# Where a fused transformer block waits for its transfers: waits on other products, queries in fewer transfers, and one PSUM bank used less

## The chip, the cores and the metric

The kernel runs on one core of a Trainium2 chip. The core has TensorE (PE; its weight loads are listed apart as PEld), VectorE (DVE), ScalarE (ACT), GpSimd (POOL) and SyncE (SP, which here does nothing but issue DMAs). TensorE writes its results to PSUM, whose banks (128 partitions of 512 fp32 values) are handed out by name. The metric is the device time of one launch in microseconds, and lower is better. A profiled execution comes with each kernel; its span is the time from its first instruction to its last, a little less than the time of the launch.

## The reference

One transformer block with adaptive layer norm: 2048 rows of 512 values, 32 attention heads of 16 with one shared key and value head, and an MLP of width 1376, all in fp32.

```python
sa, ca, ga, sb, cb, gb = split(silu(c) @ w_mod)            # six rows of 512
h = layernorm(x) * (1 + ca) + sa
q = (h @ wq) as 32 heads of 16;  k = h @ wk;  v = h @ wv   # one k, v of 16 for all heads
p = softmax(q k^T * 16 ** -0.5)
x = x + ga * ((p v) @ wo)
h = layernorm(x) * (1 + cb) + sb
x = x + gb * (gelu(h @ w1 + b1) @ w2 + b2)
```

## The kernel before, in words

**Numbers.** TensorE takes operands in a reduced fp32 format. Where that is not enough a value is split into a high and a low part and three products are summed (high x high, low x high, high x low). Queries lie in DRAM in such parts (`dq`), and a unit's query tile `qst` holds in each of its two halves (partitions 0 to 63 and 64 to 127, the index `s`): 16 partitions high, 16 low, 16 high again, and two with the negated row maxima (48, 49). The keys `ks` are laid out to match, so that one product with 64 rows sums all three, and subtracts the maximum too.

**Attention.** The rows come in 8 blocks of 256, and each block's heads in 8 groups of four. That makes 64 units. For each unit there are three kinds of product on TensorE:
- max products `m` (L490; 2048 in all, 32 a unit): scores with the queries as rows, which VectorE reduces to row maxima (L495). They run ahead of the unit that needs them. `put_max` turns the maxima, and its `send` (L534) writes them by four DMAs into rows 48 and 49 of the unit's `qst`;
- exp products `e` (L584; 2048): scores with the keys as rows, on which ScalarE takes the exponential (L587) into `p`;
- probability products `acc` (`pv`, L598; 4096, in four column groups): `va` times `p`. A row of ones in `va` yields the sums of the softmax.

`load_q` (L461, L463) fetches a later unit's queries, six DMAs of 16 partitions each and two (L463) that set the maxima's rows; there are four `qst` tiles. It is called when half of an earlier unit's max products are reduced.

**Order.** The engines run the instructions in the order in which the Python code writes them. The main loop passes over each unit's key tiles in pairs X, Y. Each pass has two half-steps: in one the e products of the half s = 1 lead, in the other the rest, and between them `end_step` issues a burst of 16 acc products of the pair before. A counter `clock` advances four times in a pass, so a half-step is two ticks. `later(n, fn)` puts a piece of code off by n ticks, `due()` runs what has come due.

**Filling.** Into the half-steps goes other work: the query projections of later blocks, and for each finished block the rest of the layer (`rest`): the attention output times wo (`wops`), the transposes of its normalised rows (`tp`), the MLP's first product (`w1ps`) and second (`w2ps`). These are generators in `queue`. A job yields the batch of products for the next half-steps, or a number of ticks until it wants to go on (`go_on`, `advance`, `take`). `rest` yields 8 ticks ahead of the transposes and 4 ahead of w1, so that the statistics on other engines can be finished; other waits of it are shorter. A half-step without filling is written by `plain`.

**PSUM.** Max products have three banks (tag `m`), e products one each of `e0`, `e1`, `e2`, acc one (`v`), and one bank, `x`, is the filling's. In a half-step without filling `plain` puts the last max product of one of its halves into `x`:

```python
if not holder and mp.has(t) and n > 1:
    other[-1] = 1.0, lambda: mp.step(t, tag="x", bufs=1)
```

**Attention output.** `fetch_half` (L717, L719) fetches a half block's output, four pairs of DMAs into the tile `os` (the output, and the softmax sums' reciprocals `drs`). Seven ticks later `norm` multiplies them on GpSimd (L733) and splits the product into `onH`, `onL` (L134). SP executes its DMAs in order; a DMA whose tile isn't free holds all behind it.

**Weights.** w1 is fetched anew for each block in pieces of 512 KB (`fetch_w1`, L747, three tiles `w1t`), three of them when `fetch_rest` runs (with the block's x, L753). `prep_w2` loads w2 once in pieces `w2f` (L1074), which GpSimd splits. `heed` notes a w1 piece with a tick, six later than its issue; `wait_early` makes an e product (one in every fourth tick, s = 0, odd pairs) wait for the first piece whose tick has come, so that the products of w1 themselves wait for less.

## Time and profile before

| | |
|---|---|
| median of 3 runs | 1591.61 us (1591.12 to 1593.79) |
| the profiled execution | 1592.94 us |
| its span | 1590.6 us |
| mean granted TensorE clock | 0.996 of full speed |
| PE busy | 1563.0 us (98%) |
| PEld busy | 1008.8 us (63%) |
| DVE busy | 1410.8 us (89%) |
| ACT busy | 1201.1 us (76%) |
| POOL busy | 667.5 us (42%) |

Times are microseconds. A group's row gives the line, engine, operation, the tiles out<-in and their shapes, then the count, the busy time and the mean of one instruction in nanoseconds, and behind it the idle time of the engine ahead of these instructions with what ended most of it. A row of the waits, "PEld m L490 <- DVE mx L495: 145.2, 363, 1.4", says who waited, for whom, for how many us, how often, and the longest. A row of the timeline begins with the time from the span's start and a duration; "x2" means that it holds two instructions in a row, and the bracket holds the idle time ahead of it and what ended it. PEq and SPq are the sequencers of PE and SP: an EVENT_SEMAPHORE there is a wait in an instruction of its own, and a DMA_DIRECT2D is a DMA being issued. Matmuls overlap one another and their ends are modelled, so the start of a weight load is the better mark of when TensorE went on.

### The profile page before, as it was taken

The page shows a single profiled execution, that of the slowest core. Times are in us where ns is not written, and L with a number is a line of the kernel's source. Part 1 is how long each engine was busy: PE and PEld are TensorE (multiplying, and loading weights), DVE is VectorE, ACT ScalarE, POOL GpSimd, SP SyncE. Part 2 cuts the span into 40 slices and gives each one's busy share as a digit, 9 for nine tenths or more (in the row PEclk, how much of TensorE's full clock was granted, in tenths as well). Part 3 has the DMA queues.
Part 4 walks back from the last instruction along what each step waited for, and adds up shares of the span by engine and source line. Part 5 has one row for each costly group of instructions (what it writes and reads, how often), then busy time and mean ns, then how long its engine had stood idle before and what let it go on. Part 6 is the DMA issues. An engine that isn't in the chain of part 4 may idle for free.

```text
span 1590.6 us, 41519 instructions
## 1 busy us (share of the span) xinstructions
PE 1563.0 (98%) x16369; PEld 1008.8 (63%) x16369; DVE 1410.8 (89%) x2473; ACT 1201.1 (76%) x2393; POOL 667.5 (42%) x1176
## 2 busy tenths in 40 slices
PE   6999999999999999999999999999999999999998
PEld 3466665557665676657666676656666576656667
DVE  7899999899999998999989999999999999999615
ACT  5577778778777887778877887778877787778853
POOL 4445434747422571246421462244612473225711
PEclk8999999999999999999999999999999999999999
DMA  7236312313020220303112120303112120212231
GB/s 250 82 113 214 105 68 70 128 39 101 17 98 31 68 69 25 103 18 107 32 49 79 54 85 22 106 14 98 43 37 89 45 96 19 95 39 63 81 134 73
DMA packets 83126, 121.62 MB, mean 76 GB/s; under 512 B 19614, under 2 KB 56222, under 8 KB 82676
## 3 DMA queue, kind: packets, MB, share of 16 engines
q1 hardware_dynamic: 82916, 118.97, 23.0%
q8 instruction: 129, 2.11, 0.6%
q14 instruction: 65, 0.53, 0.1%
q10 hardware_dynamic: 16, 0.00, 0.0%
HBM read 91.13 MB, written 27.27 MB: 74 GB/s over the span
## 4 chain that ended last, share of the span: by engine, by line
PE 88%; DVE 4%; POOL 4%; ACT 2%; DMA 1%; issue 1%; SPq 0%; POOLq 0%; DVEq 0%; ACTq 0%
PE acc L598 29%; PE m L490 21%; PE e L584 17%; PE w1ps L183 8%; PE w2ps L183 4%; DVE mx L495 3%; PE wops L183 2%; POOL xh L805 2%; PE qps L183 2%; PE w2ps L177 1%; PE w1ps L177 1%; ACT p L587 1%; PE tp L183 1%; PE kps L159 1%; POOL x L809 0%
## 5 line engine op out<-in xcount | busy, mean ns | idle before, releaser
L495 DVE TENSOR_REDUCE mx<-m 128x1 f32<-128x512 f32 x2048 | 1270.1, 681 | 101.4 <-PE m L490 73.8
L587 ACT ACTIVATE p<-e 128x512 f32<-128x512 f32 x2048 | 1067.2, 599 | 308.0 <-PE e L584 240.2
L490 PE MATMUL m<-ks,qst 64*128 64x512 f32 x2048 | 819.6, 424 | 6.1 <-ACT ks L393 2.3
L584 PE MATMUL e<-qst,ks 64*128 64x512 f32 x2048 | 739.1, 409 | 3.4 <-ACT p L587 1.5
L598 PE MATMUL acc<-p,va 128*32 128x256 f32 x8192 | 548.8, 385 | 0.0
L490 PEld LDWEIGHTS m<-ks,qst 64*128 64x128 f32 x2048 | 362.8, 184 | 168.8 <-DVE mx L495 145.2
L584 PEld LDWEIGHTS e<-qst,ks 64*128 64x128 f32 x2048 | 366.0, 184 | 91.2 <-ACT p L587 64.2
L598 PEld LDWEIGHTS acc<-p,va 128*32 128x32 f32 x8192 | 213.9, 109 | 218.9 <-issue 115.6
L183 PE MATMUL w1ps<-h2H,w1t 64*128 64x256 f32 x1232 | 236.7, 288 | 0.8
L539 POOL TENSOR_SCALAR mt<-turned 8x32 f32<-8x32 f32 x256 | 53.4, 209 | 400.6 <-DVE turned L545 388.6
L183 PEld LDWEIGHTS w1ps<-h2H,w1t 64*128 64x128 f32 x1232 | 184.1, 185 | 32.8 <-issue 23.3
L183 PE MATMUL w1ps<-h2L,w1t 64*128 64x256 f32 x616 | 169.6, 275 | 0.0
L183 PE MATMUL w2ps<-w2H,gH 64*128 64x512 f32 x286 | 118.0, 413 | 0.0
L183 PE MATMUL w2ps<-w2L,gH 64*128 64x512 f32 x286 | 117.3, 410 | 0.0
L183 PE MATMUL w2ps<-w2H,gL 64*128 64x512 f32 x286 | 117.3, 410 | 0.0
L183 PEld LDWEIGHTS w1ps<-h2L,w1t 64*128 64x128 f32 x616 | 113.5, 184 | 0.0
L906 POOL TENSOR_SCALAR tt<-tt 128x256 f32<-128x256 f32 x77 | 31.2, 405 | 162.5 <-ACT tt L905 159.3
L907 POOL TENSOR_TENSOR tt<-tt,z 128x256 f32<-128x256 f32 x77 | 57.1, 741 | 6.4
L134 POOL TENSOR_TENSOR gL<-z,gH 128x256 fp32r<-128x256 f32 x77 | 56.9, 739 | 6.4
L917 POOL TENSOR_TENSOR z<-tt,z 128x256 f32<-128x256 f32 x77 | 56.3, 731 | 6.0
L916 POOL TENSOR_TENSOR tt<-tt,z 128x256 f32<-128x256 f32 x77 | 56.8, 737 | 0.0
L183 PEld LDWEIGHTS w2ps<-w2H,gH 64*128 64x128 f32 x286 | 52.7, 184 | 5.9 <-DVE ot L953 2.5
(188 smaller groups left out, 1468.0 us busy)
## 6 DMA issues: line engine op xcount, KB each, us to landing
w1t<-dw SPq DMA_DIRECT2D x82, 512.0 KB
qst<-dq SPq DMA_DIRECT2D x384, 32.0 KB
do<-oc SPq DMA_DIRECT2D x64, 128.0 KB
dw<-w1s SPq DMA_DIRECT2D x11, 512.0 KB
xt<-in_A_x_dram SPq DMA_DIRECT2D x4, 1024.0 KB
dq<-qH SPq DMA_DIRECT2D x16, 256.0 KB
dq<-qL SPq DMA_DIRECT2D x16, 256.0 KB
x<-in_A_x_dram SPq DMA_DIRECT2D x8, 512.0 KB
```

What stands on the lines that cost most here:

```text
L134: eng_l.tensor_tensor(out=dst_l, in0=src, in1=raw(dst_h), op=ALU.subtract)
L177: nc.tensor.matmul(ps, a, b_, start=first_, stop=last_)
L183: nc.tensor.matmul(ps, a[rows], b_[rows], start=first_ and s == 0, stop=last_ and s == 1)
L490: nc.tensor.matmul(m, qsts[u][rows, j, t * P:(t + 1) * P], ks[rows, kc * 512:(kc + 1) * 512], start=True, stop=True)
L495: nc.vector.tensor_reduce(out=self.mx[u][:, i, kc:kc + 1], in_=m, axis=AX.X, op=ALU.max)
L539: nc.gpsimd.tensor_scalar(out=mt[:, g:g + 32], in0=turned[g:g + 4 * T, :], scalar1=1.0, scalar2=0.0, op0=ALU.mult, op1=ALU.add)
L584: ins = nc.tensor.matmul(e, ks[rows, kt * P:(kt + 1) * P], rhs, start=True, stop=True)
L587: nc.scalar.activation(ptiles[u, K][:, j, s, :], e, AF.Exp, scale=0.25)
L598: nc.tensor.matmul(accs[u][32 * cidx:32 * cidx + 32, :], va[:, kt, :], rhs, start=kt == 0, stop=kt == NKT - 1)
L907: nc.gpsimd.tensor_tensor(out=tt, in0=tt, in1=z, op=ALU.mult)
L916: nc.gpsimd.tensor_tensor(out=tt, in0=tt, in1=z, op=ALU.mult)
L917: nc.gpsimd.tensor_tensor(out=z, in0=tt, in1=z, op=ALU.add)
```

## The change

- The list of noted transfers and `wait_early` now cover the queries (6 ticks for s = 1, 8 for s = 0), the rows of the maxima (5) and the w1 pieces (8, the first three of a block 24). Acc products take the waits, one transfer each, in place of e products; the first acc product of a burst's first key tile takes none. `wait_early` looks for any noted transfer whose tick has come, where it looked only at the first.
- `load_q` fetches a half's queries in two DMAs in place of three: the low parts first, then the high part, written to both of its places by one DMA. The half s = 1 comes first, also where the maxima are sent.
- `fetch_half` fetches two head groups at once, and the other two four ticks later.
- A job in `queue` has a mark for a yield of over one tick. In `plain`, no max product goes to the bank `x` while a job so marked is due within two ticks.

```diff
@@ -448,6 +448,21 @@
     NU = len(units)
     qsts = {}
 
+    heeded = []
+    def heed(dma, n):
+        if not draining[0]:
+            heeded.append((clock[0] + n, dma))
+    def wait_early(ins):
+        for one in heeded:
+            if one[0] <= clock[0]:
+                heeded.remove(one)
+                tc.add_manual_dep(ins.ins, one[1].ins.name, mybir.DependencyInfo(mybir.DependencyClass.Sync, mybir.DependencyReason.DATA),
+                                  reason="a transfer that a product needs soon")
+                break
     def load_q(u):
 
         b, Q = units[u]
@@ -456,11 +471,14 @@
         h, g, a0 = r0 // BQ, Q // 2, (Q % 2) * 2
         cols = slice(r0 % BQ, r0 % BQ + w)
         assert (h, g) in sent
-        for s in range(2):
-            for r, part in ((0, 0), (16, 1), (32, 0)):
-                nc.sync.dma_start(out=raw(qst[64 * s + r:64 * s + r + 16]), in_=dq[h][g][part, a0 + s][:, :, cols])
+        for s in (1, 0):
+            low, high = (dq[h][g][part, a0 + s][:, :, cols] for part in (1, 0))
+            n = 6 if s else 8
+            heed(nc.sync.dma_start(out=raw(qst[64 * s:64 * s + 16]), in_=low), n)
+            heed(nc.sync.dma_start(out=raw(qst[64 * s + 16:64 * s + 48]), in_=high.unsqueeze(0).to_broadcast([2, 16, 2, w])), n)
             if u >= QBUFS:
-                nc.sync.dma_start(out=raw(qst[64 * s + 48:64 * s + 50]), in_=dz)
+                heed(nc.sync.dma_start(out=raw(qst[64 * s + 48:64 * s + 50]), in_=dz), n)
 
     class Max:
 
@@ -527,11 +545,11 @@
         ml = att.tile([4 * T, P], F32R, name=f"ml{u}", tag="ml", bufs=2)
 
         def send():
-            for s in range(2):
+            for s in (1, 0):
                 for r, src in ((48, mh), (49, ml)):
                     dst = qst[64 * s + r:64 * s + r + 1].rearrange("p j (t n) -> p (j t) n", n=P)
                     ring = nc.scalar if u == 0 and s else nc.sync
-                    ring.dma_start(out=raw(dst), in_=raw(src[2 * T * s:2 * T * (s + 1), :].unsqueeze(1)))
+                    heed(ring.dma_start(out=raw(dst), in_=raw(src[2 * T * s:2 * T * (s + 1), :].unsqueeze(1))), 5)
             placed.add(u)
 
         def gather():
@@ -554,20 +572,6 @@
 
     ptiles = {}
     accs = {}
-    heeded = []
-
-    def wait_for(ins, other, reason):
-        tc.add_manual_dep(ins.ins, other.ins.name, mybir.DependencyInfo(mybir.DependencyClass.Sync, mybir.DependencyReason.DATA),
-                          reason=reason)
-
-    def heed(dma, n):
-
-        heeded.append((clock[0] + n, dma))
-
-    def wait_early(ins):
-        if heeded and heeded[0][0] <= clock[0]:
-            wait_for(ins, heeded.pop(0)[1], "a weight piece")
-
     def sexp(u, K, j, s, bank):
 
         w = blocks[units[u][0]][1]
@@ -581,9 +585,7 @@
             kt, rhs = K, qst[rows, j, :]
         else:
             kt, rhs = 2 * K + j, qst[rows].rearrange("p j n -> p (j n)")
-        ins = nc.tensor.matmul(e, ks[rows, kt * P:(kt + 1) * P], rhs, start=True, stop=True)
-        if clock[0] % 4 == 2 and s == 0 and K % 2:
-            wait_early(ins)
+        nc.tensor.matmul(e, ks[rows, kt * P:(kt + 1) * P], rhs, start=True, stop=True)
         nc.scalar.activation(ptiles[u, K][:, j, s, :], e, AF.Exp, scale=0.25)
 
     def pv(u, K):
@@ -595,8 +597,10 @@
             for cidx in range(4):
                 s, j = divmod(cidx, 2)
                 rhs = pt[:, j, s, :] if w == 512 else pt[:, kt - 2 * K, s, j * w:(j + 1) * w]
-                nc.tensor.matmul(accs[u][32 * cidx:32 * cidx + 32, :], va[:, kt, :], rhs,
-                                 start=kt == 0, stop=kt == NKT - 1)
+                ins = nc.tensor.matmul(accs[u][32 * cidx:32 * cidx + 32, :], va[:, kt, :], rhs,
+                                       start=kt == 0, stop=kt == NKT - 1)
+                if kt % 2 or cidx:
+                    wait_early(ins)
 
     def finish_unit(u):
         b, Q = units[u]
@@ -712,11 +716,17 @@
         def fetch_half(hf):
             os_ = att.tile([P, 2, KD, HQ], F32, name=f"os{b}_{hf}", tag="opk", bufs=1)
             cols = slice(hf * HQ, (hf + 1) * HQ)
-            for g in range(KD):
-                src = do[b][2 * g:2 * g + 2, :, 0:16, cols].rearrange("q c r n -> (q c) r n")
-                nc.sync.dma_start(out=os_[:, 0, g, :], in_=src)
-                src = drs[b][8 * g:8 * g + 8, cols].unsqueeze(1).to_broadcast([8, 16, HQ])
-                nc.sync.dma_start(out=os_[:, 1, g, :], in_=src)
+            def fetch_heads(gs):
+                for g in gs:
+                    src = do[b][2 * g:2 * g + 2, :, 0:16, cols].rearrange("q c r n -> (q c) r n")
+                    nc.sync.dma_start(out=os_[:, 0, g, :], in_=src)
+                    src = drs[b][8 * g:8 * g + 8, cols].unsqueeze(1).to_broadcast([8, 16, HQ])
+                    nc.sync.dma_start(out=os_[:, 1, g, :], in_=src)
+            fetch_heads(range(KD // 2))
+            later(4, lambda: fetch_heads(range(KD // 2, KD)))
             oss[hf] = os_
             later(7, lambda: norm(hf))
 
@@ -744,7 +754,7 @@
 
     def fetch_w1(b, w1ts, f):
         w1ts[f] = wts_pool["rest"].tile([P, 2, KD, P], F32R, name=f"w1t{b}_{f}", tag="w1t", bufs=3)
-        heed(nc.sync.dma_start(out=raw(w1ts[f]), in_=dw1[f]), 6)
+        heed(nc.sync.dma_start(out=raw(w1ts[f]), in_=dw1[f]), 8 if f > 2 else 24)
 
     def fetch_rest(b):
 
@@ -1094,6 +1104,7 @@
             held.append(r)
         else:
             job[0] = clock[0] + max(abs(r), 1)
+            job[2] = r > 1
         return r is not None
 
     def resume():
@@ -1109,7 +1120,7 @@
                 break
 
     def put_off(*jobs):
-        queue.extend([0, job] for job in jobs)
+        queue.extend([0, job, False] for job in jobs)
 
     def take():
         advance()
@@ -1310,7 +1321,9 @@
                 a, b_, c_, d = banks
                 one = mixture(exps(s, [(K, 0, a), (K, 1, c_)]), maxes(s, n))
                 other = maxes(t, n)
-                if not holder and mp.has(t) and n > 1:
+                soon = any(planned and time <= clock[0] + 2 for time, _, planned in queue)
+                if not holder and not soon and mp.has(t) and n > 1:
                     other[-1] = 1.0, lambda: mp.step(t, tag="x", bufs=1)
                 issue(one, exps(t, [(K, 0, b_)]) + other + exps(t, [(K, 1, d)]))
 
```

In the built program the instructions of PE, DVE, ACT and POOL other than waits stand in the same order before and after (12,137 matmuls). SP issues 996 DMAs in place of 1124. On PE the waits in instructions of their own fall from 420 to 40, and 672 acc products have a wait for a DMA. The max products in bank `x` fall from 62 to 34: the 28 that move are four in each of the blocks 0 to 6, in the two half-steps without filling ahead of the transposes and the two ahead of w1.

## The prediction

> **What bounds the kernel now.** I read the page first (busy shares, chain), then the waits of TensorE's weight loads, then the instructions of single half-steps.
>
> ```profile
> span 1590.6 us, 41519 instructions
> PE 1563.0 (98%) x16369; PEld 1008.8 (63%) x16369; DVE 1410.8 (89%) x2473; ACT 1201.1 (76%) x2393; POOL 667.5 (42%) x1176
> PE 88%; DVE 4%; POOL 4%; ACT 2%; DMA 1%; issue 1%; SPq 0%; POOLq 0%; DVEq 0%; ACTq 0%
> L495 DVE TENSOR_REDUCE mx<-m 128x1 f32<-128x512 f32 x2048 | 1270.1, 681 | 101.4 <-PE m L490 73.8
> ```
>
> TensorE is busy 98% of the span and is 88% of the chain; VectorE, reducing the max products, follows at 89%. The work of neither is changed: the built program holds the same instructions on PE, DVE, ACT and POOL in the same order, on 12,137 matmuls. What changes is which PSUM bank 28 of the max products use, what TensorE waits for, and what SP issues when. So the time can change only where TensorE or VectorE stands still, and such places must be found one by one.
>
> ```profile
> PEld m L490 <- DVE mx L495: 145.2, 363, 1.4
> L490 PEldq EVENT_SEMAPHORE  x256: 51/51/692, 29.0 to 1478.0; - x128
> L584 PEldq EVENT_SEMAPHORE  x128: 51/51/1089, 76.5 to 1515.4; - x128
>   DMA w1t<-dw: 3.5, 4
> ```
>
> Most of the waiting is for a max product's bank: 145.2 us of weight-load idle, in 363 places. The two semaphore lines are waits in instructions of their own, for the query transfers, 51 ns at the median. The last row, of the exp products' line, is the only wait for a transfer that any probability-loop product shows: 3.5 us in four times, for w1 pieces.
>
> **Transfer waits moved to probability products (acc, L598).** In the built program separate semaphore instructions on PE fall from 420 to 40, and 672 acc products carry one wait each. If all 380 were on the path, 380 x 0.051 = 19.4 us would go. Two neighbouring pairs of half-steps of one shape tell otherwise:
>
> ```profile
> 801.81 0.59 PEld L598 LDWEIGHTS acc<-p,va 128*32 128x32 f32 x16 [0.24 <-issue]
> 804.67 0.16 PEld L598 LDWEIGHTS acc<-p,va 128*32 128x32 f32 x8 [0.26 <-issue]
> 813.33 0.59 PEld L598 LDWEIGHTS acc<-p,va 128*32 128x32 f32 x16 [0.24 <-PE e L584]
> 816.19 0.16 PEld L598 LDWEIGHTS acc<-p,va 128*32 128x32 f32 x8 [0.26 <-issue]
> ```
>
> The half-step from 801.81 has no extra waits, that from 813.33 has four: 2.86 us both. I count the removal at 0; the cover is the matrix work already queued, and without it the price would be those 51 ns each. The four w1 waits go: 24 ticks of 1.43 us (half a 2.85 us half-step) stand between an early piece and its wait. That is -3.5, of which 2.18 belongs to block 0, below; the rest is **-1.3**. The other new waits are 5 to 8 ticks, 7 to 11 us, behind the place where SP is given the transfer. Before has no wait for query rows anywhere, so I take 0, except where SP itself is late (block 0). 128 fewer issues help SP, which bounds nothing.
>
> **The bank left alone (x).** Max products have three banks of their own (m), and in steps without filling the third product of a step takes the filling's bank x. After the change 28 of 62 don't: four in each of blocks 0 to 6, in the two half-steps ahead of the transposes (tp) and the two ahead of w1. Block 1, ahead of tp:
>
> ```profile
> 504.86 0.59 PEld L598 LDWEIGHTS acc<-p,va 128*32 128x32 f32 x16 [0.24 <-issue]
> 506.53 0.18 PEld L490 LDWEIGHTS m<-ks,qst 64*128 64x128 f32 x1 [0.15 <-DVE mx L495]
> 507.13 0.18 PEld L490 LDWEIGHTS m<-ks,qst 64*128 64x128 f32 x1 [0.41 <-DVE mx L495]
> 507.56 0.59 PEld L598 LDWEIGHTS acc<-p,va 128*32 128x32 f32 x16 [0.24 <-issue]
> 510.18 0.59 PEld L598 LDWEIGHTS acc<-p,va 128*32 128x32 f32 x16 [0.24 <-issue]
> 511.38 0.18 PEld L183 LDWEIGHTS tp<-ident,xh 64*128 64x128 f32 x1 [0.61 <-POOL x L809]
> 504.63 8.01 DVE L495 TENSOR_REDUCE mx<-m 128x1 f32<-128x512 f32 x13
> ```
>
> VectorE runs without a break here, 13 reductions in 8.01 us, 0.62 each. The third product (506.53) sits in x, the fourth (507.13) takes the m bank that was just reduced. Without x the third takes the bank freed at 507.13 and the fourth the next, one reduction later: the acc of 507.56 moves by **+0.60**. In the next half-step the fourth product needs the reduction of that step's own first. Its load then stands at about 510.65 instead of 509.52, the acc burst 0.43 behind it (507.13 to 507.56) at 511.08, against 510.18 + 0.60: **+0.30**. In return tp needs no reduction of x: its load stands 1.20 us behind its acc, where other bursts stand 1.00 (813.33's kind): **-0.20**.
>
> Ahead of w1:
>
> ```profile
> 524.64 0.59 PEld L598 LDWEIGHTS acc<-p,va 128*32 128x32 f32 x16 [0.24 <-issue]
> 525.75 0.19 PEld L490 LDWEIGHTS m<-ks,qst 64*128 64x128 f32 x2
> 525.99 0.41 PEld L490 LDWEIGHTS m<-ks,qst 64*128 64x128 f32 x2
> 526.82 0.18 PEld L584 LDWEIGHTS e<-qst,ks 64*128 64x128 f32 x1 [0.42 <-ACT p L587]
> 527.25 0.59 PEld L598 LDWEIGHTS acc<-p,va 128*32 128x32 f32 x16 [0.25 <-issue]
> 528.41 0.18 PEld L183 LDWEIGHTS w1ps<-h2H,w1t 64*128 64x128 f32 x1 [0.57 <-issue]
> 526.41 0.69 DVE L495 TENSOR_REDUCE mx<-m 128x1 f32<-128x512 f32 x1 [0.38 <-PE m L490]
> ```
>
> The fourth product's load moves behind the first's reduction, which ends at 526.41 + 0.69 = 527.10: load about 527.14, acc at 527.57, **+0.30** on 527.25. The half-step before it has a wait for ACT at this place that covers nearly all: **+0.05**. The w1 load loses its wait for x: 1.16 us behind its acc to 1.00, **-0.16**. Together 0.60 + 0.30 - 0.20 + 0.05 + 0.30 - 0.16 = 0.89 us a block, times 7 blocks = **+6.2**. Bounds: 0 if TensorE's delay only fills time in which VectorE bounds anyway; 1.25 a block, +8.8, if tp and w1 gain nothing.
>
> **Attention output fetched in two parts, block 0.** Heads 2 and 3 of the fetch are issued four ticks later, behind the queries and w2.
>
> ```profile
> 279.22 0.57 SPq L719 DMA_DIRECT2D os<-drs  x1
> 284.73 0.84 SPq L1074 DMA_DIRECT2D w2f<-in_B_w_dram  x2
> 284.44 0.74 POOL L733 TENSOR_TENSOR os<-os 128x256 f32<-128x256 f32 x1 [0.92 <-DMA os<-drs]
> 286.40 2.38 POOL L134 TENSOR_TENSOR onL<-os,onH 128x1024 fp32r<-128x1024 f32 x1
> 292.12 3.68 SPq L1074 DMA_DIRECT2D w2f<-in_B_w_dram  x2
> 296.33 1.40 SPq L747 DMA_DIRECT2D w1t<-dw  x3
> 297.85 0.68 SPq L534 DMA_DIRECT2D qst<-mh  x1
> DMA  0696889999669796899999999831320000000020
> ```
>
> The last issue moves from 279.22 to some 283.1 (two parts of queries, now three issues each, and w2f ahead of it), so GpSimd's fourth product, 284.44, and all behind it come between 0 (if that lateness is absorbed) and 3.9 us later; I take 2.5, since this product now also waits 0.92 us for its transfer, but others precede it. SP's second w2f fetch (292.12) waits for GpSimd, and behind it on SP stand x, three w1 pieces and the max rows of the next unit but one (297.85). The last row is DMA use in 40 slices of 296 to 308 us: it falls to nothing at slice 31, 305. So the max rows land near 305 before, near 307.5 after.
>
> ```profile
> 301.90 0.18 PEld L584 LDWEIGHTS e<-qst,ks 64*128 64x128 f32 x1 [1.43 <-DMA w1t<-dw]
> 303.18 0.22 PEld L584 LDWEIGHTS e<-qst,ks 64*128 64x128 f32 x2 [0.75 <-DMA w1t<-dw]
> 304.25 0.20 PEld L598 LDWEIGHTS acc<-p,va 128*32 128x32 f32 x8 [0.65 <-issue]
> 303.30:306.70 3.40, 3.40 (x21) 1.40 (x23) 1.57 (x3) 1.09 (x2) 3.23 (x4) 0.50 0.24 74
> 306.28 0.33 PEld L584 LDWEIGHTS e<-qst,ks 64*128 64x128 f32 x1
> ```
>
> Before, the w1 waits of 1.43 + 0.75 = 2.18 us hold the max rows' users back far enough. Without them the acc burst of 304.25, which now carries the max rows' waits, comes at 302.07 and stands until 307.5: 5.4 us in place of 2.18, **+3.2**. Everything of TensorE is queued behind it. Bounds: +0.7 if the rows land at 305.0, +4.6 if 3.9 us later. The windows row has the granted clock at 0.50 for 3.40 us behind those idles (columns: length, five engines' busy time, clock, DMA share, GB/s); running half as fast it loses up to 1.7 us, and I keep it: 0, bounds -1.7 and +1.7.
>
> The first product that reads those rows is the exp product at 306.28, 2.03 us behind the acc burst; a wait there would hide 2.03 of the 5.4 us, and leave +1.2.
>
> The Trainium skill ("DMA: Bandwidth & Descriptors", Rules for kernel authors) advises to issue a transfer early and to wait on its semaphore late, after the work that can be done meanwhile. That speaks against this change: with the wait left at the last place the sum would be 2.0 us lower; elsewhere no row shows a transfer late enough for it to matter. The skill ("TensorE: Matmul & The Clock Gate", Part 1: The HAM clock gate) says that the clock halves after an idle window of about 3.4 us, free-running. The length agrees with the 3.40 us at 0.50, but here 2.18 us of idle sufficed, in two pieces; if by that rule a wait of 5.4 us costs a second window, the sum would be up to 1.7 us higher.
>
> **Sum:** -1.3 + 6.2 + 3.2 = +8.1 us. The profiled execution took 1592.94 us, 2.3 more than its span, and would take 1601.0; the median of the runs is 1.33 below it, 1591.61, so 1591.61 + 8.1 = **1599.7 us** (+0.5%). About 0.2%, 3.2 us, is what a measurement of this kernel can tell from no change.
>
> **The rivals.**
>
> *Block 0 costs nothing*: the late heads are absorbed, rows land at 305, and the half clock goes or shrinks: 0 in place of +3.2, so 1596.5. For it: GpSimd is 42% busy. Against: its products wait for os transfers already. Chance 0.15.
>
> *Faster: VectorE bounds the bank steps, so giving up x is free.* At 0.62 us, four reductions take 2.48 us of a half-step of 2.62 (507.56 to 510.18), and VectorE doesn't pause for 8.01 us; if TensorE's delay is only time that it would have spent waiting for the next reductions, the +1.25 a block disappears and the gains stay: 7 x -0.36 = -2.5, with -1.3 and block 0 between -2.5 and 0: 1586 to 1588, say 1587. It decides whether TensorE has caught up by tp's first product; the reason against is that tp's half-steps wait for VectorE little. Chance 0.12.
>
> *The terms cancel*: x costs half (+3.1), block 0 and w1 -1.3 to -3: about 1592. Chance 0.12.
>
> *Semaphore instructions were on the path*: up to -19.4, with the rest about 1580. The equal half-steps speak against it. Chance 0.03.
>
> That the change does not do what it says is excluded by the built program (420 to 40, 28 products moved).
>
> **How the numbers follow.** The forecast has 0.58, its own range +4 to +12. The range 1591 to 1604 takes in the forecast's bounds to +12, the block 0 rival and the cancelling one; left out are the two fast rivals (0.15) and some 0.05 at the top. Slower by over 0.2% (above 1594.8): 0.58 + 0.14 = 0.72. Within: 0.13. Faster: 0.15.
>
> **What would show it.** Right: the half-steps at 504.86, 507.56 and 524.64 longer by 0.6, 0.3 and 0.3 us, tp and w1 loads 1.00 behind their acc; in block 0 an acc load idle some 5 us for qst, at 302; no w1t waits. Wrong: those half-steps unchanged in length (x is free), an acc idle of under 3 us in block 0, or half-steps with removed semaphores shorter than 2.86.

## The result, and the profile after

The changed kernel takes 1605.16 us (median of 5 runs, 1603.47 to 1607.21) against 1593.79 us of the kernel before in 5 runs: 1.0072 times as long, 95% interval 1.0054 to 1.0089. That is +11.4 us (8.6 to 14.2 by the interval), where +8.1 was forecast. The profiled executions agree: 1603.83 us against 1592.94. (In the experiments below, a ratio is taken to runs of the kernel before made beside that run, with medians of 1592.92 to 1593.73 us.)

The changed kernel's page (span, busy time, chain), then its waits and the waits in instructions of their own:

```profile
span 1602.0 us, 41060 instructions
PE 1561.1 (97%) x16369; PEld 1007.0 (63%) x16369; DVE 1412.5 (88%) x2473; ACT 1203.3 (75%) x2393; POOL 665.6 (42%) x1176
PE 90%; DVE 6%; DMA 2%; POOL 1%; ACT 1%; SPq 1%; issue 0%; DVEq 0%; ACTq 0%; POOLq 0%
PEld m L508 <- DVE mx L513: 157.3, 367, 1.1
L508 PEldq EVENT_SEMAPHORE  x8: 51/51/51, 33.2 to 86.0; - x8
  DMA qst<-mh: 9.5, 2
```

TensorE does the same work in the same busy time and stands still longer. The wait for max products' banks is up by 12.1 us, and a wait for max rows (`mh`) on acc products is new: 9.5 us in two entries, which is one stall of 5.0 us seen by the weight load and again, as 4.5 us, by the matmul. The semaphore instructions of the max products fall from 256 to 8; what that was worth is read below, at a_noearly.

The half-steps of block 1 ahead of the transposes and ahead of w1, in the changed kernel (they answer to 504.86 to 511.38 and 524.64 to 528.41 before):

```profile
511.12 0.59 PEld L600 LDWEIGHTS acc<-p,va 128*32 128x32 f32 x16 [0.25 <-issue]
513.38 0.18 PEld L508 LDWEIGHTS m<-ks,qst 64*128 64x128 f32 x1 [0.72 <-DVE mx L513]
514.40 0.59 PEld L600 LDWEIGHTS acc<-p,va 128*32 128x32 f32 x16 [0.24 <-issue]
516.91 0.18 PEld L508 LDWEIGHTS m<-ks,qst 64*128 64x128 f32 x1 [0.96 <-DVE mx L513]
517.34 0.59 PEld L600 LDWEIGHTS acc<-p,va 128*32 128x32 f32 x16 [0.25 <-issue]
518.34 0.18 PEld L183 LDWEIGHTS tp<-ident,xh 64*128 64x128 f32 x1 [0.41 <-issue]
531.69 0.59 PEld L600 LDWEIGHTS acc<-p,va 128*32 128x32 f32 x16 [0.25 <-issue]
534.20 0.18 PEld L508 LDWEIGHTS m<-ks,qst 64*128 64x128 f32 x1 [0.97 <-DVE mx L513]
534.62 0.59 PEld L600 LDWEIGHTS acc<-p,va 128*32 128x32 f32 x16 [0.24 <-issue]
535.63 0.18 PEld L183 LDWEIGHTS w1ps<-h2H,w1t 64*128 64x128 f32 x1 [0.41 <-issue]
516.16 2.48 DVE L513 TENSOR_REDUCE mx<-m 128x1 f32<-128x512 f32 x4 [0.45 <-PE m L508]
```

The half-step from 511.12 takes 3.28 us (2.70 before), that from 514.40 2.94 (2.62), that from 531.69 2.93 (2.61); tp's and w1's first loads stand 1.00 and 1.01 us behind their acc, where they stood 1.20 and 1.16. VectorE, without a pause for 8.01 us before, now waits 0.45 us for a product: with one bank less, each engine waits for the other in turn.

Block 0 in the changed kernel: TensorE's loads, the transfers' issue, GpSimd, one row of the chain, and the windows view of 3.4 us in the stall and of the stretch behind it:

```profile
303.70 0.14 PEld L600 LDWEIGHTS acc<-p,va 128*32 128x32 f32 x2 [0.31 <-issue]
308.85 1.44 PEld L600 LDWEIGHTS acc<-p,va 128*32 128x32 f32 x14 [5.01 <-DMA qst<-mh]
293.48 0.18 PEld L183 LDWEIGHTS wops<-woH,onL 64*128 64x128 f32 x1 [0.69 <-POOL onL L134]
283.55 0.57 SPq L725 DMA_DIRECT2D os<-drs  x1
296.79 3.66 SPq L1084 DMA_DIRECT2D w2f<-in_B_w_dram  x2
302.50 0.65 SPq L552 DMA_DIRECT2D qst<-mh  x1
289.11 0.73 POOL L743 TENSOR_TENSOR os<-os 128x256 f32<-128x256 f32 x1 [1.17 <-DMA os<-drs]
302.50 6.31 DMA qst<-mh
303.90:307.30 3.40, 0.42 (x2) 0.00 (x0) 1.89 (x3) 0.79 (x2) 3.15 (x4) 1.00 0.99 366
309.40:312.60 3.20, 3.20 (x21) 2.00 (x19) 0.66 (x1) 0.24 (x1) 2.77 (x4) 0.51 0.07 18
```

The last heads are issued at 283.55 (279.22 before), GpSimd's last `os` product runs at 289.11 (284.44), SP's second w2 fetch at 296.79 (292.12) and the first max row at 302.50 (297.85). So these links are 4.3 to 4.7 us later than before. Not all of it is the fetch's doing: at 279 us the whole loop runs 1.4 us later in this trace than in that of before (1.03 at its start and 0.39 since, see the table below). Against TensorE's loop the links are 2.9 us late at the issue and 3.2 to 3.3 behind it; no later link makes up for any of it. The acc burst that carries the waits comes at 303.70 and stands for 5.01 us until the rows land 6.31 us after their issue; then TensorE runs at half clock.

To set runs beside each other I compare the starts of the same acc bursts in two traces. The table has the difference to the kernel before in three stretches of the loop, named by the times before (first acc burst 81.44 us): up to 279.28, block 0's part to 322.08, and the rest to 1537.10.

| kernel | first acc burst, us | to 279 | 279 to 322 | rest | sum | ratio of times (95%) |
|---|---|---|---|---|---|---|
| changed | 82.47 | +0.39 | +3.92 | +5.92 | +10.24 | 1.0072 (1.0054 to 1.0089) |
| a_bank | 83.44 | +0.25 | +4.38 | -0.92 | +3.71 | 1.0026 (1.0017 to 1.0034) |
| a_heads | 83.11 | +0.22 | -1.38 | +11.34 | +10.17 | 1.0069 (1.0055 to 1.0082) |
| a_order | 84.12 | +0.32 | +3.62 | +5.85 | +9.78 | 1.0074 (1.0060 to 1.0088) |
| a_three | 81.52 | +0.49 | -2.08 | +3.60 | +2.01 | 1.0021 (1.0008 to 1.0033) |
| b_soon | 81.89 | +0.56 | +0.30 | +7.14 | +8.00 | 1.0046 (1.0032 to 1.0060) |
| b_heads | 84.67 | +0.59 | +4.43 | +0.60 | +5.62 | 1.0046 (1.0031 to 1.0061) |
| a_noearly | 82.54 | +0.34 | +2.56 | +6.26 | +9.16 | 1.0069 (1.0054 to 1.0084) |
| c_noearly | 84.45 | +1.61 | -0.94 | -0.41 | +0.26 | 1.0001 (0.9992 to 1.0011) |
| c_long | 84.80 | +0.16 | -3.37 | -0.39 | -3.59 | 0.9997 (0.9988 to 1.0007) |
| b_w1 | 85.22 | +0.24 | -1.68 | -0.15 | -1.60 | 1.0004 (0.9995 to 1.0012) |
| d_late | 82.21 | +0.11 | -2.90 | +0.26 | -2.54 | 0.9990 (0.9979 to 1.0001) |
| e_late | 83.76 | +0.13 | -1.34 | -0.85 | -2.05 | 1.0000 (0.9991 to 1.0009) |

The first acc burst varies by 3.8 us between traces, also between kernels that are alike up to there (85.22 and 81.44), so it belongs to the execution and not to the kernel. It goes with the granted clock: the six traces whose first burst comes at 83.76 us or later have a stretch of 3.4 or 6.8 us at half clock between 47 and 73 us, the other eight have none there. The trace of before has the earliest first burst. (The +1.61 of c_noearly is of this kind too: 6.8 us at half clock right behind its first burst.) A sum of the table is therefore firmer on where time goes than a ratio is; a ratio says what it comes to.

### The profile page after: what moved, and what is told of

The parts are those of the page before. It is cut to its first block, busy times and chain, and to the rows that moved or that the text cites. A ratio compares the mean times of both kernels' runs of the same rounds, so it can differ in the third digit from the quotient of the medians.

```text
span 1602.0 us, 41060 instructions
## 1 busy us (share of the span) xinstructions
PE 1561.1 (97%) x16369; PEld 1007.0 (63%) x16369; DVE 1412.5 (88%) x2473; ACT 1203.3 (75%) x2393; POOL 665.6 (42%) x1176
## 4 chain that ended last, share of the span: by engine, by line
PE 90%; DVE 6%; DMA 2%; POOL 1%; ACT 1%; SPq 1%; issue 0%; DVEq 0%; ACTq 0%; POOLq 0%
PE acc L600 30%; PE m L508 22%; PE e L588 17%; PE w1ps L183 8%; DVE mx L513 5%; PE w2ps L183 4%; PE wops L183 2%; PE qps L183 2%; PE w2ps L177 1%; PE w1ps L177 1%; DMA xt<-in_A_x_dram 1%; PE tp L183 1%; PE kps L159 1%; DMA qst<-mh 0%; DVE st L803 0%
## 5 line engine op out<-in xcount | busy, mean ns | idle before, releaser
L508 PE MATMUL m<-ks,qst 64*128 64x512 f32 x2048 | 824.1, 425 | 17.3 <-DVE mx L513 11.1
L743 POOL TENSOR_TENSOR os<-os 128x256 f32<-128x256 f32 x28 | 20.5, 734 | 101.2 <-DMA os<-drs 99.9
```

The lines of the kernel that those rows point to most:

```text
L508: nc.tensor.matmul(m, qsts[u][rows, j, t * P:(t + 1) * P], ks[rows, kc * 512:(kc + 1) * 512], start=True, stop=True)
```

## The experiments

**a_bank: the changed kernel, the bank rule undone.**

```diff
-                if not holder and not soon and mp.has(t) and n > 1:
+                if not holder and mp.has(t) and n > 1:
```

> The changed kernel with one part undone: max products go to the filling's bank again, whatever is planned. Theory (the bank left alone costs 0.61 + 0.33 - 0.22 us ahead of the transposes and 0.09 + 0.33 - 0.19 ahead of w1, 0.95 a block in seven blocks): 6.6 us less than the changed kernel, and the six kinds of half-step as in the kernel before. Rival (the lost bank only fills time that VectorE would have bounded later): within 1 us of the changed kernel, with the half-steps shorter but others longer.

Measured 1596.99 us (12 runs), 0.0046 x 1593 = 7.3 us below the changed kernel by the ratios, and 6.84 in the table's last stretch. All six kinds of half-step are back to their lengths before. The theory's 6.6 holds, and the rival falls: nothing else became longer. Block 0 stays.

**b_soon: the kernel before with the bank rule alone.** The edit is the diff's marks in `go_on`, `put_off` and `plain`.

> The kernel before with one part of the change alone: no max product in the filling's bank while planned filling is due within two ticks. Theory: 0.95 us in each of seven blocks, 6.6 us more than before, in the same six kinds of half-step and nowhere else. Rival (the bank costs only together with the earlier waits): under 3 us.

Measured 1601.13 us, ratio 1.0046: +7.3 us, and +7.14 in the last stretch, of which 0.36 is one wait at 647.76 that the bank has no part in. The same half-steps grow by the same 0.6 and 0.33 us in each of the seven blocks. Block 1 in this kernel:

```profile
507.15 0.59 PEld L598 LDWEIGHTS acc<-p,va 128*32 128x32 f32 x16 [0.25 <-issue]
510.44 0.59 PEld L598 LDWEIGHTS acc<-p,va 128*32 128x32 f32 x16 [0.24 <-issue]
512.96 0.18 PEld L490 LDWEIGHTS m<-ks,qst 64*128 64x128 f32 x1 [0.96 <-DVE mx L495]
513.38 0.59 PEld L598 LDWEIGHTS acc<-p,va 128*32 128x32 f32 x16 [0.24 <-issue]
```

3.29 and 2.94 us, as in the changed kernel. So this part costs its price alone and whatever stands beside it: undone and done alone agree.

**a_heads: the changed kernel, all heads fetched at once.**

```diff
-            fetch_heads(range(KD // 2))
-            later(4, lambda: fetch_heads(range(KD // 2, KD)))
+            fetch_heads(range(KD))
```

> The changed kernel with one part undone: all four parts of the attention output are fetched at once. Theory (the late fetch makes GpSimd 4.7 us late, so SP's w2 fetch, w1 pieces and max rows in block 0): the max rows land some 3.8 us earlier, the acc burst's idle of 5.0 us shrinks to some 1.5, and wops no longer waits 0.6: 4 us less than the changed kernel, 5.5 if the half clock goes too. Rival (the price is the wait being on an acc product, which comes 2 us ahead of the rows' first use): 2 us less at most, with the idle still over 3 us.

Measured 1604.40 us, ratio 1.0069: no gain that can be told from none. Neither theory foresaw why. Block 0 does gain, from +3.92 to -1.38, more than the 4 us expected, and the stall at the max rows is gone with the half clock. But the last stretch loses 5.4 us. The acc products' view (idle until), and acc loads in blocks 0 and 2:

```profile
  DMA qst<-mh: 3.5, 5
  DMA qst<-dq: 3.0, 4
284.78 0.14 PEld L600 LDWEIGHTS acc<-p,va 128*32 128x32 f32 x2 [0.87 <-DMA qst<-dq]
651.24 0.14 PEld L600 LDWEIGHTS acc<-p,va 128*32 128x32 f32 x2 [0.57 <-DMA qst<-mh]
```

With eight `os` transfers ahead of them in SP's queue, the queries and max rows are not there when the acc products' leads of 5 to 8 ticks run out. Once in most blocks a half-step is 0.5 to 2.0 us longer (465.09, 647.76, 830.53, 1196.02 and 1378.41 in the times before). So the fetch in two parts pays for the early waits: the two edits belong together, and what the one saves in each block the other loses in block 0.

**a_order: the prologue's queries s = 0 first.**

```diff
-        for s in (1, 0):
+        for s in (0, 1) if draining[0] else (1, 0):
```

> The changed kernel with one part undone, in the prologue alone: the first units' queries of the half s = 0 are fetched ahead of those of s = 1. Theory (the first max product, of s = 0, waits for its queries behind those of s = 1): the first max product starts near 29.7 us in place of 33.3, and the first acc burst 1.0 to 1.3 us earlier; the time falls by as much. Rival (the 1.0 us at the first acc burst is how the input's transfers differ from run to run): no change at the first acc burst beyond 0.3 us.

Measured 1605.65 us, ratio 1.0074 against the changed kernel's 1.0072: no gain. The first max products of three kernels, in this order: before, changed, a_order:

```profile
29.73 0.47 PE L490 MATMUL m<-ks,qst 64*128 64x512 f32 x1 [1.16 <-DVE st L189]
32.53 0.79 PE L490 MATMUL m<-ks,qst 64*128 64x512 f32 x2 [2.34 <-ACT ks L393]
33.30 1.19 PE L508 MATMUL m<-ks,qst 64*128 64x512 f32 x3 [4.90 <-DVE ve L195]
31.61 0.76 PE L508 MATMUL m<-ks,qst 64*128 64x512 f32 x1 [2.96 <-DMA qst<-dq]
33.59 1.46 PE L508 MATMUL m<-ks,qst 64*128 64x512 f32 x3 [1.22 <-DMA qst<-dq]
```

The order does move the first max product, by 1.7 us here, but the second waits for the keys (`ks`, 32.53) or its own queries in any case, and the first acc burst comes at 84.12, 1.65 later than in the changed kernel's trace. Neither the theory (1.0 to 1.3 earlier) nor the rival (no change beyond 0.3) had that. This trace has 6.8 us at half clock from 64.7 us, which the changed kernel's hasn't, so the two first bursts can't be compared for the order's sake.

**a_three: bank, heads and prologue undone together.**

> The changed kernel with the three parts undone together: the bank, the fetch in two parts, the prologue's order. What is left of the change are the waits on acc products and the queries in fewer transfers. Theory (the parts add up, 6.6 + 4 to 5.5 + 1.0 to 1.3, and what is left gains some 0.4 from the w1 waits): 11.5 to 13.5 us less than the changed kernel, so within 2 us of the kernel before, likelier below it. Rival (the waits moved to acc cost or save by themselves): more than 3 us above or below the kernel before.

Measured 1598.00 us (12 runs), ratio 1.0021: 3.3 us above the kernel before (1.3 to 5.3), 8.1 below the changed one, not 11.5 to 13.5. The rest of the change, the waits on acc products, costs by itself when the heads are fetched at once: +3.60 us in the last stretch, at the same place in each block as in a_heads. By the intervals this is nearer to the rival than to the theory.

**c_noearly: the same three undone, and no acc product waits.**

```diff
-                if kt % 2 or cidx:
-                    wait_early(ins)
```

> The changed kernel with the bank, the fetch in two parts and the prologue's order undone, and no acc product waiting for a transfer: each product waits for its own, in an instruction of its own where it waits for more. What is left is the queries in fewer transfers. Theory (the waits of acc products for queries and maxima stand too early, and the waits in instructions of their own cost nothing): the half-steps that wait for queries, 0.4 to 1.7 us each, eight of them, are gone, and the early w1 waits of the kernel before too: 3 to 4 us less than the kernel before, 5 to 8 less than with acc products waiting. Rival (the 380 instructions that wait on PE cost their 51 ns): up to 19 us more than with acc products waiting.

Measured 1592.73 us (11 runs), ratio 1.0001: 3.2 us below a_three by the ratios, where 5 to 8 were expected, though the last stretch goes from +3.60 to -0.41 as it should. Against the kernel before it was to gain 3 to 4 and gained nothing. In block 0 the stalls for w1 are gone, but two half-steps from 284.5 to 289.8 (in the times before) are 1.5 and 1.2 us longer. The matmul that stands still in the first of them:

```profile
292.54 0.47 PE L508 MATMUL m<-ks,qst 64*128 64x512 f32 x1 [1.67 <-DMA qst<-dz]
```

A max product waits for the last of its queries' transfers, the two rows from `dz`, for which the kernel before waits 0.22 us at this place. Behind it the granted clock was 0.58 from 293 to 296 us, which is the second half-step's 1.2. In this order of transfers a wait of that kind takes the place of those removed.

**c_long: the same three undone, acc products wait, but later.**

```diff
-            n = 6 if s else 8
+            n = 12 if s else 14
...
-                    heed(..., 5)
+                    heed(..., 8)
```

> The changed kernel with the bank, the fetch in two parts and the prologue's order undone, and the waits on acc products later: queries 12 and 14 ticks behind their issue in place of 6 and 8, maxima 8 in place of 5. Theory (with the fetch in one part the queries are issued behind it, and their waits come before they land): the eight half-steps that are 0.4 to 1.7 us longer with the short leads, 5.8 us in the profile, are as before; 4 to 6 us less than with the short leads, and the same within 2 us as with no acc waits at all. Rival (waits on acc products cost or save by themselves): over 3 us from the kernel with no acc waits.

Measured 1592.96 us (11 runs), ratio 0.9997: 3.8 us below a_three by the ratios, 5.6 in the table, and level with c_noearly. In the table the two are 3.9 us apart, which is more than the rival's 3 us, but not by the loop's waits: the last stretch is -0.39 here and -0.41 there, and the rest is c_noearly's stall for `dz` and its half clock behind the first burst. The waits in instructions of their own in c_long, of max and of exp products:

```profile
L508 PEldq EVENT_SEMAPHORE  x218: 51/51/268, 31.3 to 1477.9; - x109
L588 PEldq EVENT_SEMAPHORE  x124: 51/51/51, 81.0 to 1515.1; - x124
```

Only the leads differ from a_three, so what a_three's acc waits cost, they cost by standing too early. But a_three has 8 and 2 of these instructions: with the longer leads the max and exp products wait for themselves again, nearly as in c_noearly (218 and 128). So the two kernels are alike in this too, and what such instructions cost is not to be read from this pair; a_noearly, next, shows it.

**a_noearly: the changed kernel, no acc product waits.** The edit is c_noearly's.

> The changed kernel with its bank rule and its fetch in two parts, and no acc product waiting for a transfer. Theory: in block 0 the first product that needs the max rows is the exp product some 2 us behind the acc burst, so the idle there is near 3 us in place of 5.0; elsewhere no change; 2 us less than the changed kernel, to 3.5 if the half clock goes too. Rival (the acc waits cover 380 waits in instructions of their own): up to 19 us more.

Measured 1603.89 us, ratio 1.0069. Block 0 costs +2.56 in place of +3.92, 1.4 us less, not 2 to 3.5. TensorE's loads and matmuls there:

```profile
307.15 0.18 PEld L183 LDWEIGHTS wops<-woH,onH 64*128 64x128 f32 x1 [2.15 <-DVE x L794]
309.23 0.76 PE L588 MATMUL e<-qst,ks 64*128 64x512 f32 x1 [1.57 <-DMA qst<-ml]
```

The wait falls apart in two: wops waits for VectorE's addition of x (the block's x stands in SP's queue behind the late w2 fetch too), and the exp product for the max rows. So the waits' place accounts for a third of block 0's price; the lateness of the transfers is most of it. The waits in instructions of their own, of max and of exp products, where the changed kernel has 8 and 2:

```profile
L508 PEldq EVENT_SEMAPHORE  x218: 51/51/51, 33.4 to 1488.3; - x109
L588 PEldq EVENT_SEMAPHORE  x128: 51/51/51, 78.3 to 1525.6; - x128
```

With those of other products TensorE's queue holds 352 such waits in the last stretch, against 13 in the changed kernel, and that stretch is +6.26 in place of +5.92. These are 0.34 us for 339 instructions of 51 ns, which would be 17.3 us on the path: the rival falls.

**b_heads: the kernel before with the fetch in two parts alone.**

> The kernel before with one part of the change alone: the attention output fetched in two parts, the second four ticks later. Six query transfers stand ahead of the second part here, where the changed kernel has four. Theory: GpSimd's last os product of block 0 comes 5 us later, SP's second w2 fetch, w1 pieces and max rows with it; the w1 waits of the exp products in block 0 (1.43 and 0.75 us before) grow by some 4.5 us together, and wops waits 0.6: 4 to 6 us more than before, all of it between 285 and 310 us. Rival (block 0's price in the changed kernel comes of the waits on acc products alone): under 1.5 us.

Measured 1599.48 us, ratio 1.0046: +7.3 us (4.9 to 9.7); by the table +5.62, of it +4.43 in block 0 and 0.6 in one half-step at 1025. The table's sum is in the range expected, the times' 7.3 lies above it, with an interval that reaches into it. The wait sits elsewhere than expected:

```profile
295.84 0.18 PEld L183 LDWEIGHTS wops<-woH,onH 64*128 64x128 f32 x1 [1.71 <-POOL onH L127]
298.27 0.29 PEld L183 LDWEIGHTS wops<-woH,onL 64*128 64x128 f32 x1 [2.13 <-POOL onL L134]
311.69 0.18 PEld L584 LDWEIGHTS e<-qst,ks 64*128 64x128 f32 x1 [1.58 <-DMA w1t<-dw]
```

The w1 waits (1.43 before) have hardly grown, since wops already stood still for GpSimd, 1.71 and 2.13 us; behind the first of these the clock is halved for 6.8 us, where the kernel before has 3.4 us of that in block 0. The late heads cost some 4 us here too, at the first wait behind them.

**b_w1: the kernel before, w1 pieces awaited later.**

```diff
-        heed(nc.sync.dma_start(out=raw(w1ts[f]), in_=dw1[f]), 6)
+        heed(nc.sync.dma_start(out=raw(w1ts[f]), in_=dw1[f]), 8 if f > 2 else 24)
```

> The kernel before with one number changed: the first three w1 pieces of a block are awaited 24 ticks after their issue in place of 6. Theory: the stalls of 1.43 and 0.75 us in block 0 go with the half clock behind them, and two of 0.2 us later; the max rows' first exp product in block 0, at 306.28, comes 2.5 us earlier and then waits up to 1 us itself: 2.5 to 4 us less than before. Rival (the max rows land at 305 whatever comes ahead, so the wait is only moved): within 1 us.

Measured 1593.86 us (11 runs), ratio 1.0004. The two stalls are gone (2.49 us in the table's steps), and the half clock with them, but the next half-step is 0.93 longer all the same, since an exp product in it waits for the max rows, longer than the 1 us expected:

```profile
308.96 0.47 PE L584 MATMUL e<-qst,ks 64*128 64x512 f32 x1 [1.81 <-DMA qst<-ml]
```

That makes -1.60 in all, and nothing visible in the times. The 0.2 us at two later places did not go here; they go in every kernel that has the queries in fewer transfers, c_noearly too. So they are not waits for w1.

**d_late: b_w1, and a block's first w1 pieces issued six ticks later.**

```diff
-        for f in range(3):
-            fetch_w1(b, w1ts, f)
         early[b] = x1, w1ts
+        def pieces():
+            for f in range(3):
+                fetch_w1(b, w1ts, f)
+        if b == len(blocks) - 1:
+            pieces()
+        else:
+            later(6, pieces)
```

> The kernel before with the w1 pieces awaited 24 ticks behind their issue and the first three pieces of a block issued six ticks later, so that in block 0 the max rows and queries go ahead of 1.5 MB of w1. Theory: in block 0 the stalls of 1.43 and 0.75 us go, and no wait for the max rows takes their place; the half clock goes too: 2.5 and 1.1 us, with 0.4 later, 4 us less than before. Rival (the pieces then come late for w1): a wait of w1 in block 0 takes back 1 us or more.

Measured 1591.14 us (12 runs), the lowest median of all; ratio 0.9990 (0.9979 to 1.0001), which doesn't quite exclude no change. In block 0 both steps give what was expected, -2.50 and -1.11 (the half clock); ahead of them two half-steps are 0.50 and 0.15 longer. The whole sum is -2.54, not the 4 us expected. The acc burst at 303.28, and the windows view of 3.4 us behind it:

```profile
303.80:307.20 3.40, 3.40 (x44) 1.81 (x36) 3.40 (x7) 2.54 (x5) 3.23 (x4) 1.00 0.23 56
303.28 0.59 PEld L598 LDWEIGHTS acc<-p,va 128*32 128x32 f32 x16 [0.30 <-issue]
```

TensorE is busy throughout, at full clock. No w1 product waits for a piece, so the rival falls.

**e_late: a_bank with the w1 pieces six ticks later.** The edit of `fetch_rest` is d_late's.

> The changed kernel with the bank undone, and the first three w1 pieces of a block issued six ticks later, as a way to keep the fetch in two parts and the acc waits without their price in block 0. Theory: the max rows are issued 1.4 us earlier and land without 1.5 MB ahead of them, some 5 us earlier, so the idle of 5.0 us at the acc burst and its half clock go: 6.6 us less than the changed kernel with the bank undone, 2 to 4 less than the kernel before. Rival (GpSimd's lateness of 4.7 us alone holds them): idle of 3 us or more at that acc burst.

Measured 1592.68 us (11 runs), ratio 1.0000: 4.1 us below a_bank, and level with the kernel before, where 2 to 4 us less were expected (the table's sum is -2.05). In block 0 it gains 5.7 us on a_bank, of the 6.6 expected:

```profile
304.63 0.58 PEld L600 LDWEIGHTS acc<-p,va 128*32 128x32 f32 x6 [0.31 <-DMA qst<-mh]
305.68 0.16 PEld L600 LDWEIGHTS acc<-p,va 128*32 128x32 f32 x8 [0.46 <-DMA qst<-ml]
309.21 0.75 PEld L600 LDWEIGHTS acc<-p,va 128*32 128x32 f32 x12 [0.97 <-DMA qst<-dq]
```

The stall, 4.91 us in a_bank, is down to 0.31 and 0.46, with 0.97 for queries behind it, and no half clock. The rival falls: 1.5 MB of w1 ahead of 8 KB of max rows was what made GpSimd's lateness dear.

## Why the prediction was right or wrong

**The direction and the two large terms were right.** Slower was forecast, by 8.1 us; it is 11.4 by the runs and 10.24 by the loop's bursts. The measured median lies 5.5 us above the forecast and 1.2 us above its range. 2.2 us come from the base: the forecast was put on a median of 1591.61 us from three runs, and five gave 1593.79; it carried no spread of the base itself, and the first acc burst alone moves by 3.8 us. About 1 us may be the start of the loop, which is 1.03 later in the changed kernel's trace. 2.1 us are in the terms. The step that failed is the w1 term, a gain of 1.3 us from waits that were not there; a wait of wops for GpSimd, worth some 0.6 us in block 0, had been put at nothing, and the bank was 0.6 us too small.

**The bank.** Forecast per block +0.60, +0.30, -0.20, +0.05, +0.30, -0.16 = 0.89. Block 1 measured +0.57, +0.33, -0.22, +0.09, +0.33, -0.18 = 0.92; seven blocks cost 6.8 (a_bank) where 6.2 was forecast. The step that decided it, that the fourth product waits for the reduction of its own half-step's first, stands in the trace as 0.96 us of idle. The rival by which VectorE bounds these half-steps fell.

**Block 0.** Forecast +3.2, measured +3.92. GpSimd's lateness was mis-sized: 2.5 taken, 3.3 measured against TensorE's loop (4.67 between the two traces, less the 1.4 us by which the whole loop is later), inside the upper bound of 3.9. From issue to landing the rows took 6.31 us, where the forecast had 7.2 (297.85 to 305). These two errors cancel, which is luck: with the 1.4 us taken off, the acc burst came at 302.3 (302.07 forecast) and the rows landed at 307.4 (307.5), and the idle was 5.01 us (5.4). The wait of wops for GpSimd, 0.69 us here, had been left out; its half-step is 0.60 longer, which is nearly all that is missing. The half clock came once in block 0 of both kernels, as taken. With the wait left at the last place the sum was to be 2.0 us lower; a_noearly shows 1.4 in block 0, since wops then waits for x.

**The w1 waits.** Forecast -1.3; with these waits alone removed, the last stretch gains 0.15 (b_w1). This step failed in the reading. "DMA w1t<-dw: 3.5, 4" adds two kinds of row: before, the same two stalls are seen by the weight load and by the matmul behind it.

```profile
301.90 0.50 PE L584 MATMUL e<-qst,ks 64*128 64x512 f32 x1 [1.00 <-DMA w1t<-dw]
303.18 0.72 PE L584 MATMUL e<-qst,ks 64*128 64x512 f32 x2 [0.32 <-DMA w1t<-dw]
```

1.43 + 0.75 + 1.00 + 0.32 = 3.5. There were two stalls, not four, and both were in block 0's term already. The last stretch of the changed kernel without its bank rule is still 0.92 us shorter (a_bank), 0.43 of it at the two places that are not waits for w1; that this comes near to the 1.3 is luck.

**Semaphore instructions at no cost:** right, by a_noearly (0.34 us for 339 of them). **Query waits at no cost:** right for the change as it stands, with the price hidden in the two-part fetch; I named the SP queue as the exception only in block 0. (Before isn't quite without waits for query rows, as I had read: 0.22 us for `dz` stand in block 0.) a_heads and a_three show that without the two-part fetch they cost 3.6 to 5.4 us.

**The clock rule.** In the changed kernel the longer idle did not bring a second half-speed stretch: 0.51 of full clock for 3.2 us behind 5.01 us of idle, against 0.50 for 3.4 behind 2.18 us before. The extra 1.7 us that the Trainium skill's page on the clock gate ("TensorE: Matmul & The Clock Gate", Part 1: The HAM clock gate) let one fear did not come there. But it came in two other traces with much the same stall, a_order (5.35 us) and a_bank (4.91 us). The last of these:

```profile
308.03:311.42 3.39, 2.11 (x14) 1.28 (x14) 0.00 (x0) 0.00 (x0) 3.22 (x4) 0.50 0.29 100
311.44:314.84 3.40, 3.40 (x15) 2.14 (x14) 2.05 (x3) 1.40 (x3) 1.45 (x2) 0.50 0.22 59
```

That half-step is 6.66 us longer there than before, and 5.90 in the changed kernel, though the stall is 0.10 shorter. The free-running window of which the Trainium skill's page speaks agrees with the traces: in each of them the half-speed stretches last 3.41 us or two or three times that, and begin whole multiples of 3.41 us apart (in the changed kernel at 29.21, 80.41 and 309.11 us, 15 and 67 multiples). So whether a stall of this length costs one stretch or two seems to depend on where it falls between these marks, which differ from one execution to the next. A window that is idle throughout isn't needed here: in the last one ahead of the half clock before, from 299.87 us, TensorE is busy for 2.08 of 3.40 us. The advice of the Trainium skill ("DMA: Bandwidth & Descriptors", Rules for kernel authors) to wait late is borne out: the same waits later, by six ticks for queries and three for maxima (c_long), gave back 3.8 us against a_three.

What stays open: where the 1 to 3 us come from by which most ratios lie above the table's sums. The sums leave out the prologue, and the trace of before has the earliest first burst. The spread goes with the clock: among the runs of one kernel, those whose mean granted clock is lower by 0.001 take some 0.9 us longer (correlation -0.77 over all runs on record). But with one trace of the kernel before, how much of the gap this is can't be shown.

## What to carry to other kernels

A spare PSUM bank is not idle because another use of it is due soon: cost the reduction that its user must then wait for (0.62 us here) against the wait that the other use loses (0.2 us). A wait put on an earlier instruction saves nothing where the waits were covered, and ties the queue's order to it: ask what stands ahead of that transfer in its queue at that tick. When small rows go behind large weights in one queue, issue the weights later: that took 5.7 us off block 0 of the changed kernel without its bank rule (e_late against a_bank). On the kernel before the same step is not shown to gain in the times (d_late, ratio 0.9990, interval to 1.0001).

## What the runs showed of the hardware that I had not expected

339 more semaphore instructions on TensorE's queue, 51 ns each, made 0.34 us of difference over 1215 us of the loop (a_noearly against the changed kernel). The half-speed stretches lie on a grid of 3.41 us that is not tied to the program: the same stall cost one stretch in one trace and two in another. And the start of the loop differs by up to 3.8 us from one execution to another (81.44 to 85.22 us), with the half-speed stretches in the prologue, which is more than most of the edits here are worth.
